# Last group of a Strassen-style FFN: one product moved forward into a PSUM bank of its own, and one of the last two stores made a single transfer

## The chip, the cores and the metric

The kernel runs on one core of one Trainium2 chip. The metric is the device time of one execution in microseconds (us); lower is better. Engine names are those of the profile: PE is the matrix engine, PEld its weight load, DVE the vector engine, ACT the scalar engine, POOL the GpSimd engine and SP the engine whose queue issues most DMA transfers. A name with a q (SPq, ACTq) is an engine's instruction queue, where DMA issues and waits are shown. "L737" is line 737 of the kernel's file.

## The reference

`q`, `k` and `v` have the shape 8 x 8 x 576 x 64 (batch, head, position, width). Cosformer attention without a mask is followed by a feed-forward layer with a leaky ReLU:

```python
r   = maximum(x, 0); phi(x) = concat(r * cos(theta), r * sin(theta))   # theta = pi/2 * pos / 576
kv  = einsum('bhsf,bhsd->bhfd', phi(k), v);  z = sum(phi(k), axis=2)
att = einsum('bhsf,bhfd->bhsd', phi(q), kv) / (einsum('bhsf,bhf->bhs', phi(q), z) + 1e-6)
x   = att as 4608 rows (batch, position) of 512 (head, width)
h   = x @ w_in                       # 512 -> 2048
out = maximum(0.01 * h, h) @ w_out   # 2048 -> 512, float32
```

## The kernel before

**Groups.** The 4608 rows are worked off in nine groups of 512. Groups 0 to 7 are the first 512 positions of one batch each. Group 8, the last, holds the remaining 64 positions of all eight batches. Within it the 128 rows of one sub-tile are the 64 tail positions of two batches that follow one another, so in the output tensor they are two runs of 64 rows, 576 rows apart.

**The second matrix product as seven products.** From group 1 on, the product with `w_out` follows Winograd's form of Strassen's scheme. The output of a group, 512 rows x 512 columns, is four quarters of 256 x 256: (row half r, column half c). Seven products of half size give them all. `product(g, n)` (L692) names the two factors of product n. One product is 16 matmuls with 128 x 256 outputs: two row sub-tiles `tt` of 128 rows, eight steps of the contraction for each (L736 to L744). `ORDER7` (L704) is the order of the seven, and `CHAIN` (L705) names the accumulator, a PSUM tile of 128 x 2 x 256 float32, that each product is added into:

```python
    ORDER7 = (1, 6, 2, 7, 5, 4, 3)
    CHAIN = {1: "X", 2: "X", 6: "Y", 7: "Y", 4: "Y", 5: "Z", 3: "Z"}
```

After product 1 the accumulator X is copied to `t1` by ACT (L756). After 2, X is quarter (0,0) and is copied to an output tile by ACT (L765). After 6, DVE makes `t2 = Y + t1`. After 7, DVE makes `t3 = Y + t1`. Product 5 gives quarter (1,1) as `Z + t3`, product 4 gives quarter (1,0) as `Y + t1`, product 3 gives quarter (0,1) as `Z + t2`. These DVE additions are all recorded under L526, the helper `tt_op`.

**The last group differs.** There the chain Z is "apart": each of its two sub-tiles has a bank of its own (the names `ps_f` in the profile) and is evicted as soon as its eight matmuls are done: one DVE addition of 128 x 256, then `store_tail`. So the products 5 and 3 leave in two parts, `tt` = 0 and 1, and the others as a whole quarter. The chain Y sits in the tile of the pool `ps_n`, and X in one of the two slots of `ps_o`. Output tiles of the last group come from the pool `stage`, which has four slots used in turn (L780). Six output tiles are made in this order: the quarter of 2, the two parts of 5, the quarter of 4, the two parts of 3. The fifth takes the slot of the first and the sixth that of the second, and the DVE addition that writes it waits until the earlier tile's stores have landed.

**The stores.** `store_quarter` (L792) writes a whole quarter of the last group with two transfers of 128 KB, one issued by SP for partitions 0 to 63, one by ACT for partitions 64 to 127. `store_tail` (L783) does the same for a part: two transfers of 64 KB. Every transfer is a list of rows of 1 KB. Each issue carries the shape of the transfer; in the kernel before, the shape of every one of its transfers starts with 64 or 128 (the partitions), for `store_tail` 64 x 256.

**What sets the order.** The kernel's schedule is written out by hand. The products of a group are woven with the first matrix product of the next group; in the last group, which has no next one, the 28 units (seven products, two sub-tiles, two halves of the contraction) stand alone and in the order of `ORDER7`. Each engine runs its instructions in the order in which they were issued in the program, and waits on semaphores for what it needs. At the end SP waits for all stores, and all engines meet at a barrier (L1201).

Of the kernel before, what the change touches and what calls it, by code (L numbers as in the profile page):

```python
# [20 lines left out]
def kernel(  # L21
# [14 lines left out]
    nc = tc.nc  # L36
    B, H, S, D = q.shape
# [3 lines left out]
    MAIN = J * P  # L41
    TAIL = S - MAIN
# [7 lines left out]
    NG = B + 1  # L50
    NE = D + 2
    G7 = 1
# [25 lines left out]
    def psum(where, shape, dtype, name):  # L78
        p = {"h": ps_h, "o": ps_o, "n": ps_n}[where]
        return p.tile(shape, dtype, name=name, tag="ps_" + where)  # L80
# [7 lines left out]
    def need(*keys):  # L88
        for key in keys:
            assert key in done, key  # L90
# [59 lines left out]
    for i in range(DFF // 512):  # L150
        for c in range(0, NKC, 2):
            t = const.tile([P, 2, 512], dt.float16, name=f"w1_{i}_{c}")
# [359 lines left out]
    NPR, HT, HC = NFT // 2, 2 * P, DM // 2  # L512
# [9 lines left out]
    t1, t2, t3 = (ext[:, 3 * HF // 2 + i * 512 :][:, 0:512] for i in range(3))  # L522
    w2q = w2.rearrange("p (i e) (n c) -> p e n i c", e=2, n=2)

    def tt_op(o, a, b, op, eng=DVE):
        eng.tensor_tensor(out=o, in0=a, in1=b, op=op)  # L526
# [142 lines left out]
    def g_sum(g, n, lo, hi, by=1):  # L669
        sl = slice(lo, hi, by)  # L670
        for i in range(lo, hi, by):
            need(*(("g", g, i, r) for r in {1: (1,), 2: (0,), 3: (0, 1), 4: (0,)}[n]))
            need(*(("S", g, i, k) for k in {1: (), 2: (1,), 3: (1,), 4: (2,)}[n]))
            done.add(("S", g, i, n))
        parts = [(tt, half) for tt in range(2) for half in range(lo // 4, (hi + 3) // 4)]
        if n == 4:
            need(*(("f2", g, 2, *x) for x in parts))
        if n == 1 and g > G7:
            need(*(("f2", g - 1, 5, *x) for x in parts))
        a11, a12, a21, a22 = (  # L680
            g_quarter(g, r, e, lo, hi, by) for r in range(2) for e in range(2)
        )
        if n == 1:
            tt_op(S1[:, sl], a21, a22, ALU.add)
        elif n == 2:
            tt_op(S2[:, sl], S1[:, sl], a11, ALU.subtract)
        elif n == 3:
            tt_op(a21, a11, a21, ALU.subtract)
        else:
            tt_op(a12, a12, S2[:, sl], ALU.subtract)  # L690

    def product(g, n):  # L692

        return {
            1: (g_quarter(g, 0, 0), w2q[:, 0, 0]),
            2: (g_quarter(g, 0, 1), w2q[:, 1, 0]),
            3: (g_quarter(g, 0, 1), w2q[:, 1, 1]),
            4: (g_quarter(g, 1, 1), T4),
            5: (S1, T1),
            6: (S2, T2),  # L700
            7: (g_quarter(g, 1, 0), w2q[:, 0, 1]),
        }[n]

    ORDER7 = (1, 6, 2, 7, 5, 4, 3)  # L704
    CHAIN = {1: "X", 2: "X", 6: "Y", 7: "Y", 4: "Y", 5: "Z", 3: "Z"}  # L705
# [3 lines left out]
    ORDER71 = (1, 2, 6, 5, 7, 4, 3)  # L709
    CHAIN1 = {**CHAIN, 2: "W", 4: "V"}  # L710

    def ffn2s(g, u, halves=(0, 1)):
        lone = g == G7
        n, tt = (ORDER71 if lone else ORDER7)[u // 2], u % 2
        a, b = product(g, n)
        key = "ps7", g, (CHAIN1 if lone else CHAIN)[n]
        apart = g == NG - 1 and CHAIN[n] == "Z"
        if apart:
            key = *key, tt
        first = key not in st  # L720
        if first:
            where = "n" if g == NG - 1 and key[2] == "Y" else "h" if apart else "o"
            if lone and key[2] == "Y":
                where = "h"
            if where == "h" and not lone:
                ps = st["H"].pop(0).rearrange("p (t c) -> p t c", t=2)
            else:
                ps = psum(where, [P, 2, HC], dt.float32, "ps_7")
            st[key] = ps
        ps = st[key]  # L730
        part = range(4 * halves[0], 4 * halves[-1] + 4)
        if n > 2:
            s, t = {3: (4, 3), 4: (3, 4), 5: (1, 1), 6: (2, 2), 7: (3, 3)}[n]
            need(("T", t), *(("S", g, i, s) for i in part if n != 4))
        need(*(("g", g, i) for i in part))
        for i in range(4 * halves[0], 4 * halves[-1] + 4):  # L736
            nc.tensor.matmul(  # L737
                ps[:, tt],
                lhsT=a[:, i, tt * P : (tt + 1) * P],
                rhs=b[:, i],  # L740
                start=(first and i == 0),
                stop=(i == NPR - 1 and (apart or tt == 1)),
                skip_group_check=True,
            )  # L744
        done.update(("f2", g, n, tt, half) for half in halves)
        if apart and halves[-1] == 1:
            part = slice(tt * HC, (tt + 1) * HC)
            osb = out_tile(g, HC)
            tt_op(osb, ps[:, tt], {5: t3, 3: t2}[n][:, part], ALU.add)
            store_tail(2 * (n == 5) + tt, 1, osb)  # L750
        if apart or tt == 0 or halves[-1] == 0:
            return
        done.add(("f2", g, n))
        flat = ps.rearrange("p t c -> p (t c)")
        if n == 1:
            nc.scalar.copy(t1, flat)  # L756
        elif n == 6:
            tt_op(t2, flat, t1, ALU.add)
        elif n == 7:
            tt_op(t3, flat, t1, ALU.add)  # L760
            if lone:
                z = st["ps7", g, "Z"].rearrange("p t c -> p (t c)")
                result(g, 5, lambda osb: tt_op(osb, z, t3, ALU.add))
        elif n == 2 and not lone:
            result(g, 2, lambda osb: nc.scalar.copy(osb, flat))  # L765
            if g not in TUNE["S4s"]:
                g_sum(g, 4, 0, NPR)
        elif n != 5 or not lone:
            t = {2: t1, 5: t3, 4: t3 if lone else t1, 3: t2}[n]
            result(g, n, lambda osb: tt_op(osb, flat, t, ALU.add))  # L770

    def result(g, n, write):
        osb = out_tile(g, 512)
        write(osb)
        r, c = {2: (0, 0), 5: (1, 1), 4: (1, 0), 3: (0, 1)}[n]
        store_quarter(g, r, c, osb.rearrange("p (t c) -> p t c", t=2))

    def out_tile(g, n):
        if g == NG - 1:
            return stage.tile([P, n], dt.float32, name="osb", tag="stage")  # L780
        return opool.tile([P, n], dt.float32, name="osb", tag="osb")

    def store_tail(tt, c, osb):  # L783
        for o in range(2):
            r0 = (2 * tt + o) * S + MAIN
            queue = ACT if o else nc.sync
            queue.dma_start(
                out[r0 : r0 + TAIL, c * HC : (c + 1) * HC],
                osb[o * TAIL : (o + 1) * TAIL, :],
            )  # L790

    def store_quarter(g, r, c, osb):  # L792
        cols = slice(c * HC, (c + 1) * HC)
# [112 lines left out]
    def f1p(g, u, n):  # L906
        return lambda: ffn1s(g, u, n)

    def f1(g, m, where="h"):
        return lambda: ffn1(g, m, where=where)  # L910

    def f2h(g, i):
        return lambda: ffn2s(g, i // 2, (i % 2,))

    def f1e(g, u, e):
        return lambda: ffn1e(g, u, e)
# [34 lines left out]
    order = [(tt, part) for part in range(3) for tt in range(J)]  # L951
# [151 lines left out]
    for g in range(NG):  # L1103
        order, seen = TUNE["O"][g + 1], {}
        lo, span = (11, 5) if g == 0 else (16 * g, 16)
        for n, c in enumerate(order):
            x = seen[c.lower()] = seen.get(c.lower(), -1) + 1
            if c == "F":
                u = f2h(g, x)
            elif c == "M":  # L1110
                u = f1(g + 1, x + 6 * (g == 0))
            elif c.isdigit():
                u = f1p(g + 1, x, int(c))
            else:
                u = f1e(g + 1, x, c)
# [90 lines left out]
```

## Time and profile before

| what | value |
|---|---|
| time, median of 3 runs | 276.06 us (275.75 to 277.05) |
| the profiled execution's own time | 276.87 us |
| its span | 275.1 us |
| granted PE clock | 1.0 |
| busy: PE, PEld, DVE, ACT, POOL | 97%, 77%, 73%, 62%, 41% |
| HBM read, written | 36.70 MB, 9.44 MB |
| DMA transfers issued by ACT (queue q10) | 608 packets, 0.52 MB |

The span is the profiled execution's length from its first to its last recorded instruction; 1.77 us of its own time lie outside. Busy shares are of the span. The DMA part of the page counts packets: a row of 1 KB is one, and so is each small closing packet.

### The profile page before, as it was taken

The page shows a single profiled execution, that of the slowest core. Times are in us where ns is not written, and L with a number is a line of the kernel's source. Part 1 is how long each engine was busy: PE and PEld are TensorE (multiplying, and loading weights), DVE is VectorE, ACT ScalarE, POOL GpSimd, SP SyncE. Part 2 cuts the span into 40 slices and gives each one's busy share as a digit, 9 for nine tenths or more (in the row PEclk, how much of TensorE's full clock was granted, in tenths as well). Part 3 has the DMA queues.
Part 4 walks back from the last instruction along what each step waited for, and adds up shares of the span by engine and source line. Part 5 has one row for each costly group of instructions (what it writes and reads, how often), then busy time and mean ns, then how long its engine had stood idle before and what let it go on. Part 6 is the DMA issues. An engine that isn't in the chain of part 4 may idle for free.

```text
span 275.1 us, 6879 instructions
## 1 busy us (share of the span) xinstructions
PE 266.3 (97%) x2813; PEld 212.5 (77%) x2813; DVE 201.5 (73%) x413; ACT 171.6 (62%) x293; POOL 112.2 (41%) x89
## 2 busy tenths in 40 slices
PE   8899999999999999999999999999999999999993
PEld 3575455557875568668999989999999999999983
DVE  4850597799964467888798878798997787667852
ACT  7756447478914476875679988756844565656400
POOL 2586002795679890440397899210510003000000
PEclk9999999999999999999999999999999999999999
DMA  7999999999699999989988997647915142211214
GB/s 223 373 393 411 383 399 370 374 365 231 207 162 245 302 218 254 289 234 231 226 293 125 272 234 208 148 114 159 183 48 128 27 101 67 69 38 40 77 44 111
DMA packets 77119, 57.59 MB, mean 209 GB/s; under 512 B 49312, under 2 KB 65696, under 8 KB 76704
## 3 DMA queue, kind: packets, MB, share of 16 engines
q1 hardware_dynamic: 76480, 56.63, 75.1%
q10 hardware_dynamic: 608, 0.52, 0.6%
q8 instruction: 22, 0.36, 0.5%
q14 instruction: 9, 0.07, 0.1%
HBM read 36.70 MB, written 9.44 MB: 168 GB/s over the span
## 4 chain that ended last, share of the span: by engine, by line
PE 78%; DMA 9%; DVE 5%; SPq 2%; POOL 2%; ACT 1%; issue 1%; ACTq 0%; DVEq 0%
PE ps L737 27%; PE ps_h L474 20%; PE ps_f L626 18%; PE ps_o L500 5%; DMA xT<-xs 4%; DMA kst<-in_k_dram 3%; PE ps_kv L326 2%; PE ps_num L400 2%; DMA qtl<-in_q_dram 2%; PE ps_f L737 1%; DVE ext L526 1%; POOL kp L253 1%; DVE xs L416 1%; SPq L363 1%; PE ps_qt L386 1%
## 5 line engine op out<-in xcount | busy, mean ns | idle before, releaser
L737 PEld LDWEIGHTS <-g 128*128 128x128 f16 x640 | 61.5, 98 | 8.3 <-DVE g L526 0.2
L737 PE MATMUL ps<-w,g 128*128 128x256 f16 x496 | 64.7, 273 | 0.1
L474 PE MATMUL ps_h<-xT,w 128*128 128x512 f16 (+1 forms) x272 | 59.0, 366 | 0.7 <-DMA xT<-xs 0.7
L474 PEld LDWEIGHTS <-w 128*128 128x128 f16 x272 | 30.0, 114 | 21.8 <-issue 0.8
L484 ACT ACTIVATE g<-ps_h 128x1024 f16<-128x1024 f32 x32 | 32.2, 1022 | 23.2 <-PE ps_h L474 23.1
L653 ACT ACTIVATE g<-ps_f 128x512 f16<-128x512 f32 x60 | 34.7, 596 | 12.9 <-DVE ps_f L526 6.2
L626 PEld LDWEIGHTS <-w 128*128 128x128 f16 x320 | 34.7, 114 | 0.8 <-issue 0.2
L626 PE MATMUL ps_f<-xT,w 128*128 128x256 f16 x240 | 34.4, 273 | 0.0
L737 PE MATMUL ps<-T,ext 128*128 128x256 f16 x240 | 31.4, 273 | 0.0
L253 POOL TENSOR_SCALAR kp<-kst,sin_t 128x256 f16<-128x256 f32 x16 | 20.6, 1295 | 21.7 <-PE ps_kv L326 21.7
L737 PEld LDWEIGHTS <-ext 128*128 128x128 f16 x256 | 24.7, 98 | 3.3
L626 PEld LDWEIGHTS <-wext 128*128 128x128 f16 x240 | 26.2, 114 | 1.2 <-issue 0.6
L253 POOL TENSOR_SCALAR qp<-qst,cos_t 128x512 f16<-128x512 f32 (+1 forms) x9 | 18.3, 2030 | 8.3 <-DMA qst<-in_q_dram 4.3
L416 DVE TENSOR_TENSOR xs<-ps_num,rden 128x512 f16<-128x512 f32 x28 | 19.4, 691 | 2.9 <-DMA xT<-xs 2.0
L253 POOL TENSOR_SCALAR kp<-kst,cos_t 128x256 f16<-128x256 f32 (+1 forms) x15 | 19.7, 1313 | 3.5 <-DMA kst<-in_k_dram 3.3
L626 PE MATMUL ps_f<-X,wext 128*128 128x256 f16 x128 | 18.9, 273 | 0.5 <-ACT ps_f L259 0.5
L526 DVE TENSOR_TENSOR osb<-ps,ext 128x512 f32<-128x512 f32 x23 | 15.7, 684 | 4.0 <-PE ps L737 3.4
L253 POOL TENSOR_SCALAR qp<-qst,sin_t 128x512 f16<-128x512 f32 (+1 forms) x9 | 18.3, 2036 | 0.0
L526 DVE TENSOR_TENSOR ext<-g 128x512 f16<-128x512 f16 (+1 forms) x23 | 14.2, 621 | 5.2 <-ACT g L484 3.4
L526 DVE TENSOR_TENSOR ps_f<-ps_f,u 128x512 f32<-128x512 f32 x20 | 13.9, 694 | 5.2 <-PE ps_f L626 2.7
L737 PE MATMUL ps<-ext,g 128*128 128x256 f16 x128 | 17.3, 273 | 0.0
L526 DVE TENSOR_TENSOR y<-ps_f,s 128x512 f32<-128x512 f32 x20 | 13.7, 687 | 3.2 <-PE ps_f L626 1.5
(118 smaller groups left out, 427.7 us busy)
## 6 DMA issues: line engine op xcount, KB each, us to landing
out_dram<-osb SPq DMA_DIRECT2D x32, 256.0 KB, 3.1
qst<-in_q_dram SPq DMA_DIRECT2D x7, 1024.0 KB, 10.3
kst<-in_k_dram SPq DMA_DIRECT2D x5, 1152.0 KB, 8.1
vst<-in_v_dram SPq DMA_DIRECT2D x5, 1152.0 KB, 7.1
w2st<-in_moe_w_out_dram SPq DMA_DIRECT2D x3, 1024.0 KB, 12.7
vst<-in_v_dram SPq DMA_DIRECT2D x4, 576.0 KB, 7.4
ext<-in_moe_w_in_dram SPq DMA_DIRECT2D x4, 512.0 KB, 10.3
kst<-in_k_dram SPq DMA_DIRECT2D x2, 576.0 KB, 8.1
```

What stands on the lines that cost most here:

```text
L253: eng.tensor_scalar(out=o, in0=i, scalar1=0.0, scalar2=col, op0=ALU.max, op1=ALU.mult)
L326: nc.tensor.matmul(ps[:, o, (c - lo) * NE : (c - lo + 1) * NE], lhsT=st["kp", b][sl, c, j, :], rhs=vm[sl, c, j, :], start=(j == 0), stop=( ...
L363: nc.sync.dma_start_transpose(out=qpT_pair(g, jp).rearrange("p o h t -> p (o h) t"), in_=st["qp2", g, jp].rearrange("p o h f -> p (o h f)"),)
L400: nc.tensor.matmul(ps[lo:hi, h // 4, (h % 4) * NE : (h % 4 + 1) * NE], lhsT=qpT[:, h, lo:hi], rhs=kv[b][:, h, :],)
L416: nc.vector.tensor_tensor(out=xs, in0=ps[:, :, 0 : 4 * NE].rearrange("p a (b e) -> p a b e", e=NE)[:, :, :, 0:D], in1=rden.rearrange("p (a ...
L474: nc.tensor.matmul(ps[:, m % 2, lo:hi], lhsT=w1[m // 4, c][0][:, w1[m // 4, c][1], m % 4 : 512 : 4], rhs=xT[:, lo // P : hi // P, c, :], s ...
L484: nc.scalar.activation(st["g", g][:, m - 1 : m + 1, :], ps, AF.Lrelu)
L500: nc.tensor.matmul(st["ps_o", g, tt], lhsT=st["g", g][:, m, tt * P : (tt + 1) * P], rhs=w2[:, m, :], start=(m == 0), stop=(m == NFT - 1),)
L526: eng.tensor_tensor(out=o, in0=a, in1=b, op=op)
L626: nc.tensor.matmul(ps[:, mi * HT : (mi + 1) * HT], lhsT=a[:, c, 2 * r0 + mi : 512 : 4], rhs=b[:, c], start=(n in (1, 5) and mi == 0 and c ...
L653: nc.scalar.activation(st["g", g][:, m : m + 2, r * HT : (r + 1) * HT], {"a": A, "c": y22, "e": E, "d": B_}[e].rearrange("p (m t) -> p m t ...
L737: nc.tensor.matmul(ps[:, tt], lhsT=a[:, i, tt * P : (tt + 1) * P], rhs=b[:, i], start=(first and i == 0), stop=(i == NPR - 1 and (apart or ...
```

## The change

For the last group only, the order of the products becomes 1, 6, 2, 7, 4, 5, 3: product 4 runs ahead of 5. Product 4 gets an accumulator V of its own instead of being added to Y; V takes a slot of the pool `ps_o`. Since Y is no longer in it, its quarter is now `V + t3` instead of `Y + t1`. In `store_tail`, the part with the number 0, which is product 3's sub-tile 0 and so the last part but one, is now written by one transfer of 128 KB, issued by SP, instead of two of 64 KB by SP and ACT. The shape of that transfer's destination is 2 x 64 x 256. The other three parts are stored as before.

```diff
+    ORDER79 = (1, 6, 2, 7, 4, 5, 3)
+    CHAIN9 = {**CHAIN, 4: "V"}
+
     def ffn2s(g, u, halves=(0, 1)):
-        lone = g == G7
-        n, tt = (ORDER71 if lone else ORDER7)[u // 2], u % 2
+        lone, last = g == G7, g == NG - 1
+        order, chain = (ORDER71, CHAIN1) if lone else (ORDER79, CHAIN9) if last else (ORDER7, CHAIN)
+        n, tt = order[u // 2], u % 2
         a, b = product(g, n)
-        key = "ps7", g, (CHAIN1 if lone else CHAIN)[n]
+        key = "ps7", g, chain[n]
...
         elif n != 5 or not lone:
-            t = {2: t1, 5: t3, 4: t3 if lone else t1, 3: t2}[n]
+            t = {2: t1, 5: t3, 4: t3 if lone or last else t1, 3: t2}[n]
             result(g, n, lambda osb: tt_op(osb, flat, t, ALU.add))
...
     def store_tail(tt, c, osb):
+        rows = out.rearrange("(t o s) d -> t o s d", o=2, s=S)
+        cols = slice(c * HC, (c + 1) * HC)
+        if tt == 0:
+            nc.sync.dma_start(rows[tt, :, MAIN:S, cols], osb)
+            return
         for o in range(2):
-            r0 = (2 * tt + o) * S + MAIN
             queue = ACT if o else nc.sync
-            queue.dma_start(
-                out[r0 : r0 + TAIL, c * HC : (c + 1) * HC],
-                osb[o * TAIL : (o + 1) * TAIL, :],
-            )
+            queue.dma_start(rows[tt, o, MAIN:S, cols], osb[o * TAIL : (o + 1) * TAIL, :])
```

## The prediction, made before the changed kernel ran

> **What bounds the kernel now.** The change touches only the last group, so I read the end of the span: first the chain of waits in time order from 255 us, then the timeline of the queues, then the DMA traffic in a few windows. The columns of the chain are start, length, engine, tile, line and count.
>
> ```profile
> 257.69 7.86 PE ps L737 x72
> 265.56 1.75 PE ps_f L737 x16
> 267.30 1.75 PE ps L737 x16
> 269.05 1.76 PE ps_f L737 x16
> 270.81 0.02 issue
> 270.83 0.42 DVE osb L526
> ```
>
> From 257.69 us on PE is without a gap: each piece begins where the one before ends. 265.56 is product 5, 267.30 product 4, 269.05 product 3; each takes 1.75 us, each sub-tile half of that. PE ends at 270.81, the last addition at 271.25. From there to 275.1 lie 3.85 us that no engine computes in. What happens there is in the timeline and in the view of one line:
>
> ```profile
> 264.45 0.68 SPq L801 DMA_DIRECT2D out_dram<-osb  x1
> 269.81 0.66 ACTq L801 DMA_DIRECT2D out_dram<-osb  x1
> 270.53 0.56 SPq L787 DMA_DIRECT2D out_dram<-osb  x1
> 271.28 0.47 SPq L787 DMA_DIRECT2D out_dram<-osb  x1
> 271.46 0.56 ACTq L787 DMA_DIRECT2D out_dram<-osb  x1
> L1201 SPq EVENT_SEMAPHORE  x7: 17/28/28, 273.8 to 275.0; - x7
> ```
>
> The last two stores are issued at 271.28 and 271.46 (ACT was still busy with the issue before). SP's first closing wait passes at 273.8, so the later store landed about 2.3 us after its issue; the barrier then takes 1.3 us, to 275.1. The end is therefore set by when the last store lands, and its traffic matters. Four queue lines follow, each from the DMA view of one window: the first of 252 to 256 us, the next two of 264.4 to 268, the last of 270 to 276. The columns are packets, MB, and their time as a share of 16 DMA engines in the window.
>
> ```profile
> q1 hardware_dynamic: 272, 0.26, 18.7%
> ```
> ```profile
> q1 hardware_dynamic: 144, 0.13, 17.3%
> q10 hardware_dynamic: 144, 0.13, 10.7%
> ```
> ```profile
> q10 hardware_dynamic: 304, 0.26, 13.3%
> ```
>
> Each store of 256 KB is 256 rows of 1 KB and 16 more packets; each of 128 KB is 128 and 16; the last line is three stores (128 + 64 + 64 rows) and 48. So each store is closed by 16 small packets whatever its size: one on each of 16 engines. The price of one row on one engine is share x 16 x window / rows: 18.7% x 16 x 4.0 / 256 = 46.8 ns for a quarter store of 128 partitions by one issue; 78 ns (q1) and 48 ns (q10) for the two halves of product 2's store, 64 partitions each; 50 ns for q10 at the end.
>
> **The change, part by part.**
>
> *Order of 4 and 5.* PE does the same 112 matmuls and ends at 270.81 as before. Product 4 now runs from 265.56 to 267.30, product 5 from 267.30 to 269.05. Product 4 needs only `g` and `T4`, both long there. Cost 0 on PE, with two covers. Product 3 adds onto the banks of 5 and must wait until DVE has read them; product 4 no longer stands between. DVE now does 4's addition from 267.34 to 268.03 (0.69, as its row of before), then 5's first part from 268.20 to 268.63 (0.42), its second from 269.07 to 269.50. Product 3 reaches the first bank at 269.05 and the second at 269.93: 0.42 us to spare each time. If DVE is late by more, PE waits for the rest.
>
> *The bank of its own.* Before, product 4 added onto Y and had to wait until DVE had read Y for `t3`; product 5 hid that wait. Now there is none. V's slot was last used by group 7's Z, read by 259.4, six us ahead. Cost 0 and gain 0, since the chain shows no wait of PE there.
>
> *What is moved in the queues.* SP's and ACT's issue of 4's two stores moves ahead of 5's four: from 269.80 to 268.06. Issues of 0.63 to 0.68 us for 4 and 0.5 to 0.8 for each part end by about 270.1 on both queues, before the next part is ready at 270.43. The 256 KB of product 4 leave 1.75 us earlier, so the traffic of the last 2 us falls from 512 rows to 256.
>
> *The output slots: a new wait.* The sixth output tile, product 3's second part, takes the slot of the second one. That was 5's first part, whose stores landed 2.0 to 2.2 us after 266.92, by 269.1. Now it is product 4's quarter, issued at 268.06. The nearest row is product 2's store, also alone on the engines: landings 2.7 us (SP) and 3.0 (ACT) after issue; 4's own row was 2.6 and 2.9. So it lands at 270.96 to 271.06, and DVE, free for the addition at 270.83, waits 0.15 to 0.25 us. Nothing is queued on DVE behind it; the last two issues wait for it, and go from 271.28 to about 271.53. ACT now is idle before its last issue, which saves the 0.18 us it came late before. The two nearly cancel: last issue at 271.53 on both queues instead of 271.46 on ACT. A part's stores landed in 2.0 to 2.2 us without neighbours against 2.3 at the end: 273.75 against 273.8. Up to here the change is worth -0.05 us, with bounds -0.45 (no wait for the slot, landing in 2.0 us after 271.28) and +0.3.
>
> *The single transfer.* It is issued by SP at 270.46 (end of its addition at 270.43, SP free since 270.0). It holds 128 rows. All other transfers of this kernel have a shape that begins with 64 or 128, and the trace shows each on 16 engines. This one's destination begins with 2, because two runs of 64 rows lie 576 apart. No row of the trace has such a store, so the cost has two ends. If it spreads over 16 engines, each gets 8 rows, as with a quarter's half, it lands within 2.7 us (273.2), ahead of the last stores, and costs nothing. If work is dealt out by the first count, only two engines get it, 64 rows each. First packets appear 1.3 us after an issue (product 2: issue 264.45, traffic from the slice at 265.75 on), so at 271.76. Each of the two engines then has 64 rows and, from the last two stores, 4 + 4 more: 72 rows. At 46.8 ns these take 3.37 us, at 50 ns 3.6, at 66 ns (q1 in the last window: 17.6% x 16 x 6 / 256) 4.75, at 78 ns 5.6. The last traffic of before is in the slice from 273.15 to 273.3, 0.5 to 0.65 ahead of SP's wait; with 0.55 for that and 1.3 for the barrier the span is 271.76 + 3.6 + 0.55 + 1.3 = 277.2 us: +2.1. By 46.8 ns it is +1.9, by 66 ns +3.3, by 78 ns +4.1. I take 50 ns: the transfer reads 128 partitions by one issue, like the quarter store of 46.8, and a little is added for the second queue. I take the two engines because the rows are cut by something, and all the shapes seen are cut into 16 by a first count that 16 divides; 2 can't be.
>
> The Trainium skill, "DMA: Bandwidth & Descriptors", section "Why a DMA increments its semaphore by 16 and not by 1", says just that: the number of engines is the largest up to 16 that divides the slowest dimension of both sides, so 128 against 2 gives two. The 16 closing packets per store agree for 64 and 128; no run here shows a 2. By the rule the sum is +2.1; without it -0.05.
>
> **The sum.** With two engines the slot's wait of 0.25 us is hidden, for the last stores queue behind the 64 rows anyway. +2.1 on the span of 275.1; the profiled execution's own 276.87 becomes 279.0. The median of the runs is 0.8 below that execution, so the prediction is 276.06 + 2.1 = 278.2 us.
>
> **The rivals.**
>
> 1. *Not slower: the transfer spreads over 16 engines* (the 64 rows of the second count are cut, or the 128 of the source). Then all that is left is -0.05 us: 276.0, at best -0.45: 275.6. For it: every one of the 96 transfers of before did use 16. Against: all began with 64 or 128. It decides if the store is closed by 16 packets spread over rows of eight per engine.
> 2. *The slot's wait becomes the end.* With 16 engines, if product 4's store lands late because 5's four stores follow it at once, DVE waits longer. At 4.4 us from issue to landing instead of 3.0 it would add 1.4 us: 277.5. For it: quarter stores of earlier groups took up to 8.2 us, among loads. Against: at the end nothing else is on the engines, and no store issued after 264 us took longer than 3.0.
> 3. *PE waits for the banks of 5.* It decides once DVE is over 0.42 us late; an addition late by a further 0.42 us, the length of one, costs as much: 276.5. DVE has nothing else to do there, so little is for it.
>
> **How the numbers follow.** About 0.5% (1.4 us) is what a measurement of this kernel can tell from no change. Two engines: 0.79. Of that nearly all lies above +1.4 us, since even 46.8 ns gives +1.9; 0.04 is left for rows that pass faster than any seen or a landing that is told sooner. Rival 1: 0.15. Rival 2: 0.03. Rival 3: 0.02. A gain of more than 1.4 us has no place to come from, since PE is without gaps and the tail's landing and barrier stay: 0.01. So slower is 0.75 + 0.02 (the part of rival 2 beyond the bound) = 0.77, same 0.04 + 0.15 + 0.01 + 0.02 = 0.22, faster 0.01. With two engines alone the range would be 277.6 to 279.8; the whole range reaches down past rival 1 to 275.8 and up to the price of 66 ns, 276.06 + 3.3 = 279.4. Left out are the higher prices and a gain.
>
> **What would show it.** Right: PE ends near 270.8 as before, the last addition starts near 271.05 and not 270.83, SP's only store between the parts of product 3 is closed by two packets and not 16, DMA traffic goes on at a low rate (two engines, some 40 GB/s) to about 275.4, and SP's closing wait passes near 275.9. Wrong: traffic stops near 273.2 at a high rate (the transfer was spread), or a gap of PE before product 3 (the banks), or a last addition far after 271.1 (the slot).

## The result and the profile after

| | before | changed |
|---|---|---|
| time, median | 276.12 us (6 runs, 275.75 to 277.05) | 278.43 us (6 runs, 277.73 to 278.97) |
| ratio, with its 95% interval | 1 | 1.0077 (1.0057 to 1.0098) |
| the profiled execution's own time, its span | 276.87, 275.1 us | 278.14, 276.4 us |
| end of PE's last matmul | 270.79 us | 270.16 us |
| from there to the end of the span | 4.3 us | 6.2 us |

The change costs 2.3 us by the medians (278.43 - 276.12). In the two profiles the part behind PE's last matmul grew by 1.9 us. The spans differ by only 1.3 us, since in the changed kernel's profiled execution PE happened to be done 0.63 us earlier. That varies from one execution to the next: in the profiles read below, whose code is the same up to the last group, PE's end lies between 269.4 and 271.4 us. So all readings of the end are taken from PE's last matmul on (end of its last group in the timeline), and this stretch is called the tail. One execution, the one profiled in e8, ran at a granted clock of 0.753 and took 346.95 us; it is left out of all comparisons.

The chain of waits of the changed kernel, at its end (start, length, engine, tile, line, count):

```profile
266.67 0.76 PE ps_f L743 x7
267.43 2.89 DMA out_dram<-osb
270.32 0.03 issue
...
270.51 0.42 DVE osb L526
```

The last addition no longer follows PE. It follows the landing of product 4's store, issued at 267.43 and landed 2.89 us later; that is the new wait on the output slot. From landing to addition another 0.19 us pass. The addition starts 0.35 us after PE's end (270.16), where before it was 0.04.

The last issues in the timeline, and SP's closing waits in the view of the closing line:

```profile
269.84 0.63 SPq L795 DMA_DIRECT2D out_dram<-osb  x1
270.97 0.49 SPq L799 DMA_DIRECT2D out_dram<-osb  x1
270.97 0.50 ACTq L799 DMA_DIRECT2D out_dram<-osb  x1
```
```profile
L1210 SPq EVENT_SEMAPHORE  x7: 17/28/185, 274.9 to 276.3; - x7
```

SP and ACT issue the last part's two stores at the same moment, as expected, yet SP's closing waits begin to pass only at 274.9, 3.9 us after them; before, they did so 2.3 us after the later of the two. What they wait for is in the page's queues (packets, MB, share) and in the traffic from 270 to 278 us in slices of 0.2 us:

```profile
q1 hardware_dynamic: 76530, 56.70, 74.2%
...
q10 hardware_dynamic: 528, 0.46, 0.5%
```
```profile
GB/s 292 220 267 215 10 31 20 51 46 15 41 36 46 36 51 102 189 282 139 67 51 41 51 15 0 0 0 0 0 0 0 0 0 41 0 0 0 0 0 0
```

The same slices of the kernel before:

```profile
GB/s 0 0 0 0 0 92 215 159 174 328 359 328 313 251 266 139 0 0 0 0 0 0 0 0 0 0 0 41 0 0 0 0 0 0 0 0 0 0 0 0
```

ACT's queue lost 80 packets (608 to 528), the 64 rows and 16 closing packets of the transfer that it no longer issues. SP's queue won 50 (76480 to 76530): the 64 rows came over, its own 16 closing packets went, and 2 came. So the single transfer is closed by 2 packets and runs on two engines. In the traffic it is the low plain between the two hills: 15 to 51 GB/s from 271.0 to 273.0, where before the stores left at up to 359 GB/s. That is the rate of two engines: two of them with 50 ns a row would move 2 x 1024 B / 50 ns = 41 GB/s. The second hill is the last part's rows on the other engines, done at about 273.8; the low end behind it, to 274.8, is again the two engines.

### The profile page after: what moved, and what is told of

It reads as the page before. It is cut to its first block, busy times and chain, and to the rows that moved or that the text cites. A ratio compares the mean times of both kernels' runs of the same rounds, so it can differ in the third digit from the quotient of the medians.

```text
span 276.4 us, 6877 instructions
## 1 busy us (share of the span) xinstructions
PE 265.2 (96%) x2813; PEld 212.3 (77%) x2813; DVE 201.2 (73%) x413; ACT 171.8 (62%) x293; POOL 112.2 (41%) x89
## 3 DMA queue, kind: packets, MB, share of 16 engines
q1 hardware_dynamic: 76530, 56.70, 74.2%
## 4 chain that ended last, share of the span: by engine, by line
PE 80%; DMA 9%; DVE 6%; POOL 2%; issue 1%; SPq 1%; ACT 0%; DVEq 0%
PE ps L743 28%; PE ps_f L626 20%; PE ps_h L474 20%; PE ps_o L500 5%; DMA kst<-in_k_dram 3%; DMA xT<-xs 2%; PE ps_num L400 2%; PE ps_kv L326 2%; DMA qst<-in_q_dram 2%; DVE ext L526 1%; DMA out_dram<-osb 1%; POOL kp L253 1%; DVE xs L416 1%; PE ps_qt L386 1%; DVE osb L526 1%
## 5 line engine op out<-in xcount | busy, mean ns | idle before, releaser
L253 POOL TENSOR_SCALAR kp<-kst,sin_t 128x256 f16<-128x256 f32 x16 | 19.3, 1214 | 21.7 <-PE ps_kv L326 21.7
L253 POOL TENSOR_SCALAR kp<-kst,cos_t 128x256 f16<-128x256 f32 (+1 forms) x15 | 20.3, 1358 | 3.2 <-DMA kst<-in_k_dram 2.9
```

Source lines behind the costliest of these rows:

```text
L253: eng.tensor_scalar(out=o, in0=i, scalar1=0.0, scalar2=col, op0=ALU.max, op1=ALU.mult)
```

## The experiments

Each edit is to the changed kernel, e2's to the kernel before. Theory 1 is the prediction's: the single transfer runs on two DMA engines, and that is the loss. Theory 2: the late use of the output slot, which the new order brings, pushes the end. Theory 3: it is the single issue by one queue that is slow. The tails at a glance, each from one profiled execution; "engines" are those of product 3's first part, and each ratio is to executions of the kernel before in the same series (medians 276.12, 275.96 and 276.13 us):

| kernel | engines | tail, us | ratio to before (95%) |
|---|---|---|---|
| before | 16 | 4.3 | 1 |
| changed | 2 | 6.2 | 1.0077 (1.0057 to 1.0098) |
| e1 order only | 16 | 4.3 | 1.0012 (0.9995 to 1.0029) |
| e2 single transfer only | 2 | 7.4 | 1.0103 (1.0082 to 1.0124) |
| e3 order, slot free | 16 | 4.1 | 0.9997 (0.9983 to 1.0010) |
| e4 both parts single | 2 | 8.7 | 1.0158 (1.0135 to 1.0182) |
| e5 two issues | 2 | 6.5 | 1.0083 (1.0067 to 1.0099) |
| e6 two issues | 4 | 4.9 | 1.0025 (1.0008 to 1.0042) |
| e12 two issues | 8 | 4.5 | one execution each: 276.85 us against 276.31 |
| e7 single on an earlier part | 16 (2 for product 5's first) | 6.4 | 1.0070 (1.0053 to 1.0087) |
| e8, e11 single, slot free | 2 | 6.1 (e11) | 1.0074 (1.0051 to 1.0097) (e8) |

**e1: the order alone.**

```diff
-        if tt == 0:
-            nc.sync.dma_start(rows[tt, :, MAIN:S, cols], osb)
-            return
```

> The changed kernel with only the new order and the bank of its own: all four parts are stored by two transfers again. Theory 1 (the single transfer runs on two DMA engines, and that is the whole loss): the span ends 4.2 to 4.4 us after PE's last matmul, as before (4.3), not 6.2 as after; the median is 275.8 to 276.4 us; the last addition still waits about 0.3 us for the landing of product 4's store. Theory 2 (the later use of the output slot by the new order pushes the end, and the single transfer is hidden): 6 us or more after PE's last matmul, median about 278.3.

Measured: tail 4.3 us, median 276.31. The chain still shows the wait for the slot:

```profile
268.15 2.89 DMA out_dram<-osb
...
271.24 0.42 DVE osb L526
```

The last addition comes 0.35 us after PE's end (270.89), exactly as late as in the changed kernel, and still the end is that of before. Theory 2 falls. The order is worth nothing that can be measured: the wait takes back what the emptier queues give.

**e2: the single transfer alone**, in the order of before.

```diff
+        if tt == 0:
+            rows = out.rearrange("(t o s) d -> t o s d", o=2, s=S)
+            nc.sync.dma_start(rows[tt, :, MAIN:S, c * HC : (c + 1) * HC], osb)
+            return
```

> The kernel before with only the single transfer for product 3's first part; order and banks as before. Theory 1: two engines get 64 rows of it, behind them 8 of the last part and ahead of them 16 of product 4's quarter, 88 x 47 ns = 4.1 us from the first traffic near 271.1: the span ends 6.2 to 6.6 us after PE's last matmul, median 278.0 to 278.6 us, the last addition without a wait for a landing. Theory 2: 4.3 us after PE's last matmul, median 276.1.

Measured: tail 7.4 us, median 278.99 against 275.96; the last addition starts without a wait for a landing. So the transfer alone does all of the damage and more, which is theory 1. But the tail is 0.8 us longer than the upper end that was expected. The traffic from 270 us in slices of 0.2:

```profile
GB/s 0 0 82 220 159 159 348 307 51 20 15 20 31 36 36 87 159 282 216 56 51 46 46 51 36 26 26 20 26 10 0 0 0 0 0 0 0 0 0 41
```

Between the hills it starts at 15 to 20 GB/s, below the 41 of two engines at 50 ns a row, and from 275.0 on at most 26 are left: about half the rate, for 0.9 us. The trace's records of the single packets show why: one of the two engines begins at 271.69 and passes most rows 42 ns apart, while the other begins at 271.87 and needs 1.14 us for its first four rows (starts at 271.87, 272.16, 272.46 and 272.76). Later it is as fast as the first, but it ends 0.95 us behind it and works alone at the end.

**e3: the order alone, and a free slot.** On top of e1's edit:

```diff
-        osb = out_tile(g, 512)
+        osb = out_tile(0 if n == 4 else g, 512)   # product 4: a tile of the other pool
```

> The new order and bank, two transfers for each part, and product 4's output tile from the other pool of output tiles, so that the last addition has no store to wait for. Both theories expect the last addition right after PE's last matmul (0.02 us instead of 0.33). Theory 1: the end moves with it, 3.9 to 4.1 us after PE's last matmul, median 275.6 to 276.1. Theory 2: against the order alone 2 us faster.

Measured: the last addition 0.09 us after PE's end, tail 4.1 us, median 275.90. Freeing the slot gives 0.26 us of tail against e1 (4.07 against 4.34), just what the addition gains. It is the fastest version here, but its ratio to before, 0.9997 (0.9983 to 1.0010), can't be told from no change.

**e4: the last part by one transfer as well.**

```diff
-        if tt == 0:
+        if tt < 2:
```

> The changed kernel with the last part stored by one transfer too. Theory 1: the same two engines get 64 + 64 rows instead of 64 + 8, 56 x 47 ns = 2.6 us more: the span ends 8.6 to 9.0 us after PE's last matmul, median 280.7 to 281.3 us. Theory 2: within 0.3 us of the changed kernel (278.4).

Measured: tail 8.7 us, 2.5 more than the changed kernel; median 280.54, just below the expected range. With 128 rows on each of the two engines instead of 72, 56 more, that is 44 ns for each, so the cost grows by the row, as theory 1 has it.

**e5: two issues, two engines.** Each run is given as 2 x 32 rows:

```diff
-            nc.sync.dma_start(rows[tt, :, MAIN:S, cols], osb)
+            for o in range(2):
+                queue = ACT if o else nc.sync
+                queue.dma_start(
+                    rows[tt, o, MAIN:S, cols].rearrange("(b a) d -> a b d", a=2),
+                    osb[o * TAIL : (o + 1) * TAIL, :],
+                )
```

> The changed kernel, but product 3's first part is stored by two transfers again, one by SP and one by ACT, each given as 2 x 32 rows (even rows of the run first, then odd ones) instead of 64; the 64 rows of each run are thereby written in another order, which leaves the traffic as it is. Theory 1 (the first count of the shape sets the number of engines): the two engines get 32 + 32 rows and 8 of the last part, 72 as in the changed kernel; the span ends 6.0 to 6.6 us after PE's last matmul, median 278.0 to 279.0 us. Theory 3 (one issue by one queue for 128 rows is what is slow, whatever its shape): as with the order alone, 4.3 us after PE's last matmul, median 276.3.

Measured: tail 6.5 us, median 278.29. The page's queues:

```profile
q1 hardware_dynamic: 76466, 56.63, 75.5%
...
q10 hardware_dynamic: 594, 0.52, 0.6%
```

Both queues have 14 packets fewer than before: each of the two stores has 2 closing packets instead of 16. The work is split over SP and ACT as before the change, the number of issues is that of before, and the loss is there all the same. Theory 3 falls.

**e6 and e12: four and eight engines**, e5 with `a=4` and `a=8`.

> The same with each transfer given as 4 x 16 rows (again the rows of a run in another order). Theory 1: four engines get 16 + 16 rows and 8 of the last part; 32 rows x 47 ns = 1.5 us are done about when the last part's rows arrive, so the end moves by 0.1 to 0.3 us against the order alone: 4.4 to 4.6 us after PE's last matmul, median 276.3 to 276.8. Theory 3: 4.3 us, median 276.3.

> Product 3's first part by two transfers, each given as 8 x 8 rows (the rows of a run in another order). If the first count sets the number of engines, each transfer is closed by 8 packets instead of 16, so the page counts 8 packets fewer on each queue than before; eight engines get 8 + 8 rows and 8 of the last part, 24 x 47 ns = 1.1 us, and the span ends as with the order alone, 4.2 to 4.5 us after PE's last matmul. Were the loss that of the row order, it would be as with two engines, 6.5.

Measured: e6 has 12 packets fewer on each queue (4 closing packets), a tail of 4.9 us and a median of 276.85, both a little above what was expected. e12 has 8 fewer (8 closing packets) and a tail of 4.5 us, as expected. So the loss against 16 engines is 2.2 us with two, 0.5 with four and 0.2 with eight: it goes with the rows per engine, and not with the order of the rows, which all three changed.

The Trainium skill, "DMA: Bandwidth & Descriptors", section "Why a DMA increments its semaphore by 16 and not by 1", gives the number of engines as the largest up to 16 that divides the slowest dimension on both sides. The closing packets agree for all four: 16, 8, 4 and 2.

**e7: the single transfer earlier.**

```diff
-        if tt == 0:
+        if tt == 2:   # product 5's first part
```

> The changed kernel with the single transfer on another part: product 5's first one, issued about 1.7 us earlier; product 3's first part leaves by two transfers. Theory 1: the two engines get 16 rows of product 4, 64 of this part and 8 of each of the three parts that follow, 104 x 47 ns = 4.9 us from about 1.45 us ahead of PE's last matmul on: the last packet 3.4 us after it (4.5 in the changed kernel, 2.6 with the order alone), the span 5.0 to 5.4 us after it, median 277.0 to 277.6. If the cost were in the place next to last alone, it would be 4.3 us and 276.3.

Measured: tail 6.4 us, median 278.07. The measured tail fits neither theory's number. The place next to last is not what counts, but 1.7 us more of lead hid nothing, where about 1 us of the loss should have gone. The traffic, from 269 us in slices of 0.2, has the same two marks as e2's:

```profile
GB/s 189 195 164 282 364 87 15 20 26 26 36 36 61 102 179 287 323 307 343 307 210 51 51 46 51 31 26 21 26 20 10 0 0 0 0 0 0 0 0 0
```

It begins at 15 to 26 GB/s right behind the first hill, product 4's rows, and ends with 1.0 us at half the rate. The packet records show the same as in e2: one engine needs 1.15 us for its first four rows (from 270.35 on), while the other begins at 270.13 and is done 0.98 us earlier.

**e8 and e11: the single transfer with the slot free**, e3's edit on the changed kernel.

> The changed kernel with product 4's output tile from the other pool, so that the last addition has no store to wait for. Theory 1: the last addition comes 0.3 us earlier, but its stores queue behind the 64 rows on the two engines: the span still ends 6.1 to 6.3 us after PE's last matmul, median 278.1 to 278.7. Theory 2 (the wait for the slot pushes the end): 0.3 us or more earlier than the changed kernel.

> The changed kernel with product 4's output tile from the other pool, once more, for its profile: the last addition 0.05 us and not 0.35 after PE's last matmul, and yet the span ends 6.1 to 6.3 us after PE's last matmul, as in the changed kernel (6.2), since the last stores queue behind the 64 rows. If the wait for the slot counted, it would be 5.9.

e11 is the kernel of e8 again, and the tail is read from e11's profile. Measured: ratio 1.0074 in e8, against 1.0077; in e11 the last addition 0.09 us after PE's end and a tail of 6.1 us. The wait for the slot is hidden behind the 64 rows, but for 0.1 us.

**e9 and e10: the single transfer by itself.** Left out are the stores of product 4, of both parts of 5 and, in e9 alone, of the last part.

```diff
+        if g == NG - 1 and n == 4:
+            return
...
+        if tt > 1:
+            return
```

The first two lines stand in `result`, ahead of the store. The last two are e10's and stand in `store_tail`; e9 has a plain `return` in their place, so that only the part with the number 0 is stored.

> The changed kernel without the stores of product 4, of both parts of 5 and of the last part (these rows of the output are left unwritten), so that the single transfer is alone on the DMA engines. Two stores with a two-engine transfer ended about 1 us later than 47 ns for each row gave; the traffic began at 15 to 36 GB/s and only later ran at 41 to 51. Theory A (the slow stretch comes from the neighbours' rows): 41 to 51 GB/s from the first slice on, 64 x 47 ns = 3.0 us of traffic, the span 5.7 to 5.9 us after PE's last matmul. Theory B (a transfer on two engines begins slowly by itself): the first microsecond at 15 to 36 GB/s, 3.4 us of traffic or more, 6.1 us or more.

> The changed kernel without the stores of product 4 and of both parts of 5 (left unwritten); the single transfer and the two of the last part are kept. Theory A: nothing is ahead of the single transfer, but 8 rows per engine of the last part come between: 41 to 51 GB/s, slower only where the last part's rows pass, the span 6.0 to 6.3 us after PE's last matmul. Theory B: slow in its first microsecond as alone, 6.4 us or more.

Measured: tails of 5.6 us (e9) and 5.9 (e10), a little below theory A's and well below theory B's. The traffic of e9, from 269 us in slices of 0.2, holds nothing but the single transfer:

```profile
GB/s 0 0 0 0 0 0 0 0 0 0 20 20 46 46 31 41 36 46 5 41 51 46 46 51 51 46 31 0 0 0 0 0 0 0 0 0 0 0 0 0
```

Some 3.3 us of traffic: 51 ns for each of the 64 rows. Theory A was wrong in form: there are pauses in the first 1.8 us without any neighbour (20 GB/s, 5 GB/s), and the even 41 to 51 comes only after that. From 272.9 to 274.3 the mean is 48 GB/s, 43 ns for a row on each of the two engines. Theory B has the pauses right, but they cost 0.3 us against 47 ns a row (0.5 against 43) and not 1, and in e9 both engines have them and end within 0.04 us of each other. So the missing microsecond of e2 and e7, the four slow rows of one engine, does not appear where the transfer is alone. What e2 and e7 share, and the changed kernel doesn't have, is that the single transfer is issued right behind product 4's two stores. Whether that is the cause, and why one engine then falls behind, was not settled.

## Why the prediction was right

*PE's end unchanged, and the cover of 0.42 us for the banks of 5.* Right: PE ends between 269.4 and 271.4 us in all the profiles read here, with the old order and with the new, without a gap ahead of product 3. Rival 3 did not happen.

*The slot.* Right in mechanism, short in size. The landing took 2.89 us, inside the 2.7 to 3.0 taken from product 2's row. What was left out is the 0.19 us between the landing and the start of the addition; the addition came 0.35 us after PE's end (0.35 to 0.40 in all runs with this wait) instead of 0.15 to 0.25. That it would nearly cancel with the emptier queues is shown by e1 (tail 4.3 as before), that it is hidden with two engines by e11 (6.1 against 6.2). Rival 2 did not happen.

*The single transfer on two engines.* Right: 2 closing packets instead of 16. This was the step on which all hung; what rival 1 (16 engines) would have given is seen nearest in e1, where the same rows leave over 16 engines by two issues: no change.

*The price of a row, 50 ns.* Right in size for this kernel, but not for the reason given: from its first traffic at 271.06 us to its last at about 274.7 lie 3.65 us for 72 rows, 50.7 ns each, against 3.6 us in the sum. By itself (e9) a row costs 51 ns in the mean. Where the transfer runs evenly it is 43 ns, less than the lower end of 46.8 (the records of such rows take 46 ns each but start 42 ns apart, so a price added up from recorded times is a little too high), and pauses of about half a microsecond make up the rest; the prediction had 46.8 ns and "a little" for the second queue, and no pauses. So luck has a part in it. It has another: the price holds for a transfer that follows other parts' stores, and where it follows product 4's quarter directly (e2, e7) the same kind of sum is short by about 1 us.

*The sum.* +2.1 us was forecast, +1.9 stands in the tail of the one profiled execution and +2.3 between the medians. In the tail the first traffic comes 0.90 us after PE's end (0.95 in the sum) and the traffic takes 3.65 us (3.6). From the last packet to the end of the span it is 1.64 us, where the sum had 0.55 + 1.3 = 1.85: this is the 0.2 us that the tail is short. 278.2 us was predicted and 278.43 measured; that they lie so near is in part chance, since the tail and the medians miss +2.1 by 0.2 us on opposite sides.

## What to carry to other kernels

When a store is merged into one transfer, look at the first count of its shape on both sides: two runs of rows that do not join make the merged transfer begin with 2, and it then runs on two DMA engines, at 64 rows x 50 ns instead of 4 or 8 rows. The saved issue did not make up for that: two issues over 16 engines (e1) beat one over two by 1.9 us of tail. In all these runs the count of closing packets in the queue's line, 16, 8, 4 or 2, told how many engines a transfer had; and a reordering that changes which output slot is used again can put a store's landing ahead of a computation.

## What was not expected of the hardware

- A transfer on two engines doesn't start evenly even alone: 5 to 46 GB/s in its first 1.8 us, then 41 to 51 (e9).
- Issued right behind two stores of 128 KB, such a transfer ended about 1 us later than its rows cost elsewhere: one of its two engines took 1.14 to 1.15 us for its first four rows and worked alone for the last 0.95 to 0.98 us (e2, e7). Why is open.
- The two halves of product 2's store, 64 partitions each, issued by SP and ACT, did not cost the same per row before the change: 78 ns and 48 ns. The cause of that was not tried.
